# Experts with 64-column weight blocks as the stationary operand, and the ranking lists of units 20 to 23 in another buffer

## The chip, the cores and the metric

The kernel runs on one core of a Trainium2 chip. The metric is device time in microseconds (us): before the change the median of three runs is 560.91 us, from 559.71 to 563.14. Five engines work in parallel, each through its own queue of instructions in order: PE (matmuls; PEld is its load of the stationary operand), DVE, ACT and POOL (element work), and SP, which only starts transfers. Transfers run on 16 DMA engines. In a matmul a stationary operand (`lhsT`) of up to 128 columns is loaded into the array and a moving operand (`rhs`) streams past it, so that the output has as many partitions as the stationary operand has columns. All arrays here are float32.

## The reference, cut to what matters

```
for t in range(S):                       # attention, state of 40 x 40 for each batch and head
    y[t]  = r[t] @ state
    state = state * w[t] - (state @ a[t]) outer b[t] + v[t] outer k[t]
x = y as rows of 320, 3072 tokens
logits = x @ w_gate                      # 8 experts, top 1
probs  = softmax(logits); each token goes to its best expert with weight gate_w
for e in range(8):
    tok = tokens of expert e; if more than 80: the 80 with the greatest gate_w
    out[tok] = gate_w[tok] * (relu(x[tok] @ w1[e]) @ w2[e])     # w1: 320 x 1024, w2: 1024 x 320
all other rows of out are 0
```

## The kernel before, in words

**Attention.** The sequence is cut into 24 units (64 steps, two batches each). Each unit's work is recorded in a planner, `Plan`, which lists all instructions in an order by their estimated costs and due times; the list is then issued, so each engine's order is fixed. This stage fills the span up to about 425 us. Its matmuls are mostly blocks of 64 by 64 (`psv_go`, `u_go`, `score`): four of them, in the four quarters of the array, follow each other in the program. `gate` computes a unit group's expert weights, and `rows_go` (L817) writes the group's rows of x to DRAM.

**Ranking.** For each expert the 80 greatest gate weights are wanted. `extract` takes eight maxima at a time (L846, L848), `merge` joins sorted lists. `rank_late` treats units 20 and 21, `rank_last` units 22 and 23; each first turns the gate weights into a list of 256 columns, `pair_a` and `pair_b` (L824, L839), which before the change lie in the two buffers named `raww`. All buffers of attention and ranking belong to the pool `hold`; `tops`, `gates` and `ids` belong to `const`.

**Weights.** When `hold` has been given back, `wpool` takes its place, and SP starts the transfers of the eight experts one after the other (L978, L980, L981): `w1` (1024 KB), `w1r`, the last 64 of the 320 rows of w1, in two halves (2 x 128 KB), and `w2` (1280 KB). That is 20.97 MB for all; every expert has tiles of its own, so that no transfer waits for the experts' work.

**Choice of tokens.** L1010 to L1051 turn the lists into a threshold, and the threshold into each expert's 80 row numbers (`idx_g`, `idx_s`).

**Experts.** POOL gathers the rows of each expert (L1063). For each expert: `turn_x` transposes them (three PE transposes, L1074 and L1075, then a DVE copy to `xe`); `first_layer` has `xe` (80 columns) stationary and lets `w1` stream past in pieces of 512 columns, four matmuls over 128 rows (L1085) and two over 64 rows, in the upper and the lower half of the array (L1088), then ReLU on ACT; `turn_h` transposes h (80 x 1024) by eight PE transposes (L1100) and two DVE copies; `second_layer` has a piece of the turned h stationary and lets `w2` stream past, eight matmuls of 320 columns (L1108); DVE multiplies by the gate weight (L1110) and POOL scatters the rows to `out` (L1111). The tile framework decides the final order on each engine and puts in the waits.

Of the kernel before, what the change touches and what calls it, by code (L numbers as in the profile page):

```python
# [145 lines left out]
def kernel(  # L146
# [77 lines left out]
    with ExitStack() as p1:  # L224
# [599 lines left out]
        pair_a, pair_b = at("raww", NM), at("raww", NM + 1)  # L824
# [4 lines left out]
        def turn_gates(pieces, dst, key, z, bis):  # L829
            kc = ("gp", pieces[0][0])  # L830
            rows = pieces[0][1] * E

            def go():
                for j, (m0, nu) in enumerate(pieces):
                    nc.tensor.transpose(ps[0:rows, bank(kc), 128 * j : 128 * j + 128],
                                        gates[:, m0 : m0 + nu, :].rearrange("p m e -> p (m e)"), ident)
            addr("PE", 0.2 * len(pieces), 0.2, z, go, [("gates", b_) for b_ in bis], (), (kc, 1))
            addr("DVE", 0.25 + 0.001 * 128 * len(pieces), 0.1, z,
                lambda: nc.vector.tensor_copy(dst, ps[0:rows, bank(kc), 0 : 128 * len(pieces)]), [kc], [key])  # L839
# [55 lines left out]
        def rank_late():  # L895
            ranked.append(1)
            z = 22 * PER
            turn_gates([(20, 1), (21, 1)], pair_a[0:E, 0:256], ("raww", NM), z, [5])
            clear_tail(z)
            extract(la[0:E], pair_a[0:E, 0:256], z, ("raww", NM), LA)  # L900
            merge(8, tops[0], tops[0], z, A0, A0)

        def rank_last():
            ranked.append(1)
            z = 24 * PER
            turn_gates([(22, 1), (23, 1)], pair_b[0:E, 0:256], ("raww", NM + 1), z, [6])
            extract(tops[1], pair_b[0:E, 0:256], z, ("raww", NM + 1), ("tops", 1))
# [151 lines left out]
    rows, xes, hs, hts = {}, {}, {}, {}  # L1059
# [18 lines left out]

    def first_layer(e):
        w1, w1r, _ = weights[e]  # L1080
        xe = xes.pop(e)
        hp = [ps_h.tile([cap, FH], F32, name="hp", tag=f"h{j}") for j in range(2)]
        for i in range(2):
            for j in range(2):
                nc.tensor.matmul(hp[j], lhsT=xe[:, i, :], rhs=w1[:, i, FH * j : FH * j + FH], start=i == 0, stop=False)  # L1085
        for j in range(2):
            half = slice(64 * j, 64 * j + 64)
            nc.tensor.matmul(hp[j], lhsT=xe[half, 2, :], rhs=w1r[half, :], start=False, stop=True)  # L1088
        hs[e] = fs.tile([cap, F], F32, name="h", tag="h")
        for j in range(2):  # L1090
            nc.scalar.activation(hs[e][:, FH * j : FH * j + FH], hp[j], Act.Relu)  # L1091

    def turn_h(e):
        h = hs.pop(e)
        hts[e] = fs.tile([128, FK, cap], F32, name="hT", tag="hT")
        for j in range(2):
            tp = ps_t.tile([128, FK // 2, cap], F32, name="tp", tag=f"t{j}")
            for f in range(FK // 2):
                o = FH * j + 128 * f
                nc.tensor.transpose(tp[:, f, :], h[:, o : o + 128], ident[:cap, :cap])  # L1100
            nc.vector.tensor_copy(hts[e][:, FK // 2 * j : FK // 2 * (j + 1), :], tp)  # L1101

    def second_layer(e):
        w2 = weights[e][2]
        hT = hts.pop(e)
        yp = ps_y.tile([cap, DM], F32, name="yp", tag="y")
        for f in range(FK):
            nc.tensor.matmul(yp, lhsT=hT[:, f, :], rhs=w2[:, f, :], start=f == 0, stop=f == FK - 1)  # L1108
        y = fs.tile([cap, DM], F32, name="y", tag="y")
        nc.vector.tensor_scalar_mul(y, yp, rows[e][:, DM : DM + 1])  # L1110
# [7 lines left out]
    for e in range(E + 1):  # L1118
        if e < E:
            first_layer(e)  # L1120
        if e + 1 < E:
            turn_x(e + 1)
        if e > 0:
            second_layer(e - 1)
        if e < E:
            turn_h(e)
# [26 lines left out]
```

## Time and profile before

| | |
|---|---|
| median of three runs | 560.91 us |
| profiled execution: its own time | 561.64 us |
| its span, first to last instruction | 559.6 us |
| PE busy in the span | 425.6 us (76%) |
| mean granted TensorE clock | 0.891 |
| bytes moved in the span | 72.91 MB |

A row of a timeline begins with the start and the length in us; equal instructions that follow each other on an engine are put together with their count. One float32 matmul of the program stands in the trace as two matmul instructions, with a load each; a PE transpose stands as one. Matmuls overlap, and each has an own length of 0.2 us and more after its operand has begun to stream; so the pace of a stream is read from start to start, not from lengths. Numbers in square brackets in a row are idle time before it, and what ended that.

### The profile page before, as it was taken

How to read it: one execution, taken by the hardware profiler on the slowest of the kernel's cores; microseconds unless marked ns; L12 is line 12 of the kernel's file. 1: busy time of each engine (PE TensorE's matmuls, PEld its weight loads, DVE VectorE, ACT ScalarE, POOL GpSimd, SP SyncE). 2: the span in 40 equal slices, each digit the busy share in tenths (PEclk: the TensorE clock that was granted, in tenths of full speed). 3: DMA queues.
4: the chain of work that ended last, by engine and by line, in shares of the span. 5: the costliest groups of instructions: out<-in, count | busy, mean ns of one | idle time of the engine just before them, and what ended most of it. 6: DMA issues, size and time to landing. Idle time of an engine off the chain costs nothing. (4 is left out here: it accounts for less than half of the span.)

```text
span 559.6 us, 22079 instructions
## 1 busy us (share of the span) xinstructions
PE 425.6 (76%) x9617; PEld 331.6 (59%) x9617; DVE 312.5 (56%) x706; ACT 186.0 (33%) x361; POOL 224.1 (40%) x393
## 2 busy tenths in 40 slices
PE   2644089797928988889799998998895003999996
PEld 2543078686717877778687887887784002344443
DVE  4867977444703855684476644966678981121211
ACT  2432064353512453444443643445231000101010
POOL 7010011788388410898699516981000005010101
PEclk9978569798976999999899999999699555899999
DMA  8775367556593477676577374327200049999300
GB/s 133 113 116 112 64 154 133 99 94 133 96 243 81 99 174 134 149 132 117 133 143 172 100 132 116 75 44 161 71 16 27 23 143 342 326 332 344 104 15 16
DMA packets 241444, 72.91 MB, mean 130 GB/s; under 512 B 217908, under 2 KB 235716, under 8 KB 241348
## 3 DMA queue, kind: packets, MB, share of 16 engines
q1 hardware_dynamic: 211428, 65.50, 51.6%
q10 hardware_dynamic: 29152, 4.36, 4.9%
q0 software_dynamic: 768, 1.64, 1.0%
q8 instruction: 76, 1.25, 0.9%
q14 instruction: 20, 0.16, 0.1%
HBM read 53.26 MB, written 18.13 MB: 128 GB/s over the span
## 5 line engine op out<-in xcount | busy, mean ns | idle before, releaser
L498 POOL TENSOR_TENSOR tmp<-lt 128x30 f32<-128x30 f32 (+9 forms) x150 | 84.0, 560 | 61.0 <-DMA lt<-blocks 50.3
L500 POOL TENSOR_TENSOR lt<-lt,tmp 128x30 f32<-128x30 f32 (+9 forms) x150 | 88.8, 592 | 11.8
L707 DVE TENSOR_TENSOR UL<-ps,mask 128x832 f32<-128x832 f32 x24 | 24.5, 1022 | 54.0 <-PE ps L702 54.0
L758 PE MATMUL ps<-wsel,xT 128*128 128x192 f32 x192 | 40.7, 360 | 2.3 <-DVE xT L748 1.4
L1111 POOL DMA_INDIRECT out_dram<-y,idx_s x8 | 7.3, 917 | 74.6 <-DVE y L1110 74.6
L758 PEld LDWEIGHTS ps<-wsel,xT 128*128 128x128 f32 x192 | 34.2, 208 | 4.3 <-DVE xT L748 1.7
L369 DVE TENSOR_TENSOR_SCAN P<-dec,begins 128x520 f32<-128x520 f32 x24 | 31.4, 1313 | 9.4 <-ACT dec L365 9.3
L1108 PE MATMUL yp<-w,hT 128*80 128x320 f32 x128 | 35.9, 434 | 0.5 <-DVE hT L1101 0.5
L344 PE MATMUL ps<-ident,raww 128*128 128x128 f32 x88 | 16.6, 320 | 25.5 <-DMA raww<-in_w_dram 24.4
L344 PE MATMUL ps<-ident,kb 128*128 128x128 f32 x192 | 32.8, 297 | 3.6 <-DVE ends L373 1.8
L735 DVE TENSOR_TENSOR st<-ps,st 128x832 f32<-128x832 f32 (+1 forms) x24 | 23.8, 990 | 17.9 <-PE ps L724 17.9
L485 POOL MEMSET nt<- 32x1024 f32 x12 | 11.3, 945 | 54.6 <-ACT nt L417 54.2
L377 DVE TENSOR_TENSOR_SCAN iv<-dec,ends 128x520 f32<-128x520 f32 x24 | 30.2, 1259 | 4.0 <-ACT ivc L396 3.3
L1085 PE MATMUL hp<-w,xe 128*80 128x512 f32 x64 | 31.6, 641 | 0.5 <-DVE xe L1077 0.5
L452 DVE TENSOR_TENSOR psi<-ps,mask 128x512 f32<-128x512 f32 x24 | 16.4, 686 | 27.3 <-PE ps L437 23.0
L1091 ACT ACTIVATE h<-hp 80x512 f32<-80x512 f32 x16 | 8.6, 587 | 61.5 <-PE hp L1088 61.5
L611 ACT COPY rv<-ps 128x1024 f32<-128x1024 f32 x24 | 24.3, 1014 | 11.4 <-PE ps L344 6.5
L344 PEld LDWEIGHTS ps<-ident,raww 128*128 128x128 f32 x88 | 11.5, 162 | 27.4 <-DMA raww<-in_w_dram 15.1
L1108 PEld LDWEIGHTS yp<-w,hT 128*80 128x80 f32 x128 | 18.6, 150 | 14.7 <-issue 0.8
L344 PEld LDWEIGHTS ps<-ident,kb 128*128 128x128 f32 x192 | 22.8, 149 | 7.4 <-issue 3.7
L407 DVE TENSOR_TENSOR kb<-rawkb,ps 128x640 f32<-128x640 f32 x22 | 17.9, 813 | 15.5 <-PE ps L344 13.4
L1077 DVE COPY xe<-xp 128x240 f32<-128x240 f32 x8 | 3.3, 407 | 40.9 <-PE xp L1075 40.9
(171 smaller groups left out, 961.3 us busy)
## 6 DMA issues: line engine op xcount, KB each, us to landing
w<-in_moe_w_dram SPq DMA_DIRECT2D x8, 1280.0 KB
w<-in_moe_w_dram SPq DMA_DIRECT2D x8, 1024.0 KB, 16.4
VL<-in_v_dram SPq DMA_DIRECT2D x96, 40.0 KB, 2.3
out_dram<-zero SPq DMA_DIRECT2D x8, 480.0 KB, 4.2
raww<-in_w_dram SPq DMA_DIRECT2D x44, 80.0 KB, 2.8
rawkb<-in_k_dram SPq DMA_DIRECT2D x44, 80.0 KB, 3.6
rawkb<-in_b_dram SPq DMA_DIRECT2D x44, 80.0 KB, 3.2
rawr<-in_r_dram ACTq DMA_DIRECT2D x84, 40.0 KB, 2.9
```

The lines of the kernel that those rows point to most:

```text
L344: nc.tensor.matmul(o, lhsT=i, rhs=ident, start=True, stop=True, is_transpose=True, skip_group_check=True)
L369: nc.vector.tensor_tensor_scan(at("P", n), at("dec", n)[:, 0 : H * SEG], begins, 0.0, op0=Alu.mult, op1=Alu.add)
L377: nc.vector.tensor_tensor_scan(at("iv", n)[:, H * SEG : 0 : -1], at("dec", n)[:, H * SEG : 0 : -1], at("ends", n)[:, H * SEG : 0 : -1], 0. ...
L407: nc.vector.tensor_tensor(out=view(at("kb", n), 0, (HB * H, 2), (HB, H), (1, D)), in0=view(at("rawkb", n), 0, (DM, 2), (D, H), (1, D)), in ...
L498: e.tensor_tensor(out=tv, in0=t3[:, 0:s, s : s + 1].to_broadcast([128, s, n]), in1=t3[:, s : s + 1, s + 1 :].to_broadcast([128, s, n]), op ...
L500: e.tensor_tensor(out=t3[:, 0:s, s + 1 :], in0=t3[:, 0:s, s + 1 :], in1=tv, op=Alu.add)
L611: nc.scalar.copy(at("rv", n).rearrange("p (k c) -> p k c", k=2), ps[:, bank(kr) : bank(kr) + 2, :])
L707: nc.vector.tensor_tensor(out=view(at("UL", n), 0, (M4 * X, 2), (1, M4 * X)), in0=view(ps[:, bank(ku), :], 0, (512, 2), (1, M4 * X)), in1= ...
L735: nc.vector.tensor_tensor(out=view(st, o, (BS, M4), (step, 2), (1, n_)), in0=view(flat, 512 * bank(ky) + o, (4 * T, M4), (step, 2), (1, n_ ...
L758: nc.tensor.matmul(ps[:, b0, WS * m : WS * m + WX], lhsT=at("xT", n)[:, 2 * T * cof(m, 0) : 2 * T * cof(m, 0) + 2 * T], rhs=wsel_[:, WS * ...
L1085: nc.tensor.matmul(hp[j], lhsT=xe[:, i, :], rhs=w1[:, i, FH * j : FH * j + FH], start=i == 0, stop=False)
L1108: nc.tensor.matmul(yp, lhsT=hT[:, f, :], rhs=w2[:, f, :], start=f == 0, stop=f == FK - 1)
```

## The change

The two lists of units 20 to 23 now lie in `begins`, a constant of the attention stage that is no longer read by then; the copy into a list is recorded as a write of `begins`, too. In the experts the roles of the operands are exchanged: blocks of 64 columns of `w1`, `w1r` and `w2` are stationary, and `xe` (80 columns) or the turned h (80 columns) moves. Even blocks write partitions 0 to 63 of a PSUM tile, odd ones 64 to 127. The first layer then gives h already turned, so that `turn_h` goes; ReLU is now split between ACT (`hp[0]`) and DVE (`hp[1]`). The second layer gives y turned, and a new `turn_y` turns it back: a DVE copy to `yT`, two PE transposes, and one matmul with `pair`, two 64 x 64 identities above one another, which adds the two halves of y's last 64 columns (their even pieces are summed in one half, their odd ones in the other). `pair` is made by two POOL copies ahead of the gathers.

```diff
@@ -821,7 +821,7 @@
             add(*args, sooner=LISTS[len(ranked)], **kw)
 
         ranked = []
-        pair_a, pair_b = at("raww", NM), at("raww", NM + 1)
+        pair_a, pair_b = begins[:, 0:256], begins[:, 256:512]
 
         def clear_tail(z):
             addr("POOL", 0.4, 0.1, z, lambda: nc.gpsimd.memset(la[:, capr:], 0.0), (), [("la", 0)])
@@ -836,7 +836,8 @@
                                         gates[:, m0 : m0 + nu, :].rearrange("p m e -> p (m e)"), ident)
             addr("PE", 0.2 * len(pieces), 0.2, z, go, [("gates", b_) for b_ in bis], (), (kc, 1))
             addr("DVE", 0.25 + 0.001 * 128 * len(pieces), 0.1, z,
-                lambda: nc.vector.tensor_copy(dst, ps[0:rows, bank(kc), 0 : 128 * len(pieces)]), [kc], [key])
+                lambda: nc.vector.tensor_copy(dst, ps[0:rows, bank(kc), 0 : 128 * len(pieces)]), [kc],
+                 [key] + [("begins", 0)] * (key[0] == "pair"))
 
         def extract(dst, src, z, src_key, dst_key):
             cols = src.shape[-1]
...
@@ -895,16 +896,16 @@
         def rank_late():
             ranked.append(1)
             z = 22 * PER
-            turn_gates([(20, 1), (21, 1)], pair_a[0:E, 0:256], ("raww", NM), z, [5])
+            turn_gates([(20, 1), (21, 1)], pair_a[0:E, 0:256], ("pair", 0), z, [5])
             clear_tail(z)
-            extract(la[0:E], pair_a[0:E, 0:256], z, ("raww", NM), LA)
+            extract(la[0:E], pair_a[0:E, 0:256], z, ("pair", 0), LA)
             merge(8, tops[0], tops[0], z, A0, A0)
 
         def rank_last():
             ranked.append(1)
             z = 24 * PER
-            turn_gates([(22, 1), (23, 1)], pair_b[0:E, 0:256], ("raww", NM + 1), z, [6])
-            extract(tops[1], pair_b[0:E, 0:256], z, ("raww", NM + 1), ("tops", 1))
+            turn_gates([(22, 1), (23, 1)], pair_b[0:E, 0:256], ("pair", 1), z, [6])
+            extract(tops[1], pair_b[0:E, 0:256], z, ("pair", 1), ("tops", 1))
 
         def late_adds():
             def late_consts():
@@ -1056,7 +1057,10 @@
     ps_h = ctx.enter_context(tc.tile_pool(name="ps_h", bufs=2, space=PSUM))
     ps_t = ctx.enter_context(tc.tile_pool(name="ps_t", bufs=1, space=PSUM))
     ps_y = ctx.enter_context(tc.tile_pool(name="ps_y", bufs=1, space=PSUM))
-    rows, xes, hs, hts = {}, {}, {}, {}
+    rows, xes, hts, yts = {}, {}, {}, {}
+    pair = fs.tile([128, HB], F32, name="pair", tag="pair", bufs=1)
+    nc.gpsimd.tensor_copy(pair[0:HB], ident[0:HB, 0:HB])
+    nc.gpsimd.tensor_copy(pair[HB:], ident[HB:, HB:])
 
     def gather(e):
         rows[e] = fs.tile([cap, XW], F32, name="rows", tag="rows", bufs=8)
@@ -1076,38 +1080,48 @@
         xes[e] = fs.tile([128, 3, cap], F32, name="xe", tag="xe")
         nc.vector.tensor_copy(xes[e], xp)
 
+    QF, NB = FK // 2, FH // 64
+
     def first_layer(e):
         w1, w1r, _ = weights[e]
         xe = xes.pop(e)
-        hp = [ps_h.tile([cap, FH], F32, name="hp", tag=f"h{j}") for j in range(2)]
+        hp = [ps_h.tile([128, QF, cap], F32, name="hp", tag=f"h{j}") for j in range(2)]
         for i in range(2):
             for j in range(2):
-                nc.tensor.matmul(hp[j], lhsT=xe[:, i, :], rhs=w1[:, i, FH * j : FH * j + FH], start=i == 0, stop=False)
-        for j in range(2):
-            half = slice(64 * j, 64 * j + 64)
-            nc.tensor.matmul(hp[j], lhsT=xe[half, 2, :], rhs=w1r[half, :], start=False, stop=True)
-        hs[e] = fs.tile([cap, F], F32, name="h", tag="h")
-        for j in range(2):
-            nc.scalar.activation(hs[e][:, FH * j : FH * j + FH], hp[j], Act.Relu)
-
-    def turn_h(e):
-        h = hs.pop(e)
+                for b in range(NB):
+                    c = 64 * (b % 2)
+                    nc.tensor.matmul(hp[j][c : c + 64, b // 2, :], lhsT=w1[:, i, FH * j + 64 * b : FH * j + 64 * b + 64],
+                                     rhs=xe[:, i, :], start=i == 0 and b < 2, stop=False, skip_group_check=True)
+        for b in range(NB):
+            c = 64 * (b % 2)
+            for j in range(2):
+                half = slice(64 * j, 64 * j + 64)
+                nc.tensor.matmul(hp[j][c : c + 64, b // 2, :], lhsT=w1r[half, 64 * b : 64 * b + 64],
+                                 rhs=xe[half, 2, :], start=False, stop=True, skip_group_check=True)
         hts[e] = fs.tile([128, FK, cap], F32, name="hT", tag="hT")
-        for j in range(2):
-            tp = ps_t.tile([128, FK // 2, cap], F32, name="tp", tag=f"t{j}")
-            for f in range(FK // 2):
-                o = FH * j + 128 * f
-                nc.tensor.transpose(tp[:, f, :], h[:, o : o + 128], ident[:cap, :cap])
-            nc.vector.tensor_copy(hts[e][:, FK // 2 * j : FK // 2 * (j + 1), :], tp)
+        nc.scalar.activation(hts[e][:, 0:QF, :], hp[0], Act.Relu)
+        nc.vector.tensor_scalar_max(hts[e][:, QF:, :], hp[1], 0.0)
 
     def second_layer(e):
         w2 = weights[e][2]
         hT = hts.pop(e)
-        yp = ps_y.tile([cap, DM], F32, name="yp", tag="y")
+        yp = ps_y.tile([128, 3, cap], F32, name="yp", tag="y", bufs=2)
         for f in range(FK):
-            nc.tensor.matmul(yp, lhsT=hT[:, f, :], rhs=w2[:, f, :], start=f == 0, stop=f == FK - 1)
+            for b in (0, 1, 2, 3, 4) if f % 2 == 0 else (1, 0, 3, 2, 4):
+                c = 64 * ((b + f) % 2) if b == 4 else 64 * (b % 2)
+                nc.tensor.matmul(yp[c : c + 64, b // 2, :], lhsT=w2[:, f, 64 * b : 64 * b + 64], rhs=hT[:, f, :],
+                                 start=f == 0 and b < 2, stop=f >= (FK - 2 if b == 4 else FK - 1), skip_group_check=True)
+        yts[e] = fs.tile([128, 3, cap], F32, name="yT", tag="yT")
+        nc.vector.tensor_copy(yts[e], yp)
+
+    def turn_y(e):
+        yT = yts.pop(e)
+        yq = ps_t.tile([cap, DM], F32, name="yq", tag="yq")
+        for i in range(2):
+            nc.tensor.transpose(yq[:, 128 * i : 128 * i + 128], yT[:, i, :], ident)
+        nc.tensor.matmul(yq[:, KW:], lhsT=yT[:, 2, :], rhs=pair, start=True, stop=True, skip_group_check=True)
         y = fs.tile([cap, DM], F32, name="y", tag="y")
-        nc.vector.tensor_scalar_mul(y, yp, rows[e][:, DM : DM + 1])
+        nc.vector.tensor_scalar_mul(y, yq, rows[e][:, DM : DM + 1])
         nc.gpsimd.indirect_dma_start(
             out=out[:, :], out_offset=bass.IndirectOffsetOnAxis(ap=idx_s[:, e : e + 1], axis=0),
             in_=y[:, :], element_offset=0, bounds_check=N - 1, oob_is_err=False, in_offset=None)
@@ -1120,10 +1134,11 @@
             first_layer(e)
         if e + 1 < E:
             turn_x(e + 1)
+        if e > 1:
+            turn_y(e - 2)
         if e > 0:
             second_layer(e - 1)
-        if e < E:
-            turn_h(e)
+    turn_y(E - 1)
 
 
 # ---- launch: one core; inputs and outputs as the reference has them ----
```

The scheduler's order on PE (before, around the second expert): the operands' names stand after the operation, `w_1` is w1 of expert 1, `x4` a count of matmuls, and "waits" names the semaphores of the engines or transfers that are waited for.

```order
L1085 MATMUL hp<-w_1_7002,xe 80x512 [waits DMAHW5_49,DVE_49]
L1085 MATMUL hp<-w_1_7002,xe 80x512 x3
L1088 MATMUL hp<-w1r_7003,xe 80x512 [waits DMAHW6_49]
L1088 MATMUL hp<-w1r_7003,xe 80x512 [waits DMAHW7_49]
L1074 MATMUL xp<-ident,rows 128x80 [waits DMASW2_49,PE_49]
L1074 MATMUL xp<-ident,rows 128x80
L1075 MATMUL xp<-ident,twice 128x80
L1108 MATMUL yp<-w_0_6997,hT 80x320 [waits DMAHW4_49,DVE_49]
```

And in the changed kernel, for the fourth and fifth expert:

```order
L1093 MATMUL hp<-xe,w_3_7016 64x80 x31
L1099 MATMUL hp<-xe,w1r_7017 64x80 [waits DMAHW6_49]
L1099 MATMUL hp<-xe,w1r_7017 64x80 [waits DMAHW7_49]
L1099 MATMUL hp<-xe,w1r_7017 64x80 x14
L1078 MATMUL xp<-ident,rows 128x80 [waits DMASW4_49,PE_49]
L1078 MATMUL xp<-ident,rows 128x80
L1079 MATMUL xp<-ident,twice 128x80 [waits Activation_49]
L1121 MATMUL yq<-ident,yT 80x128 [waits DVE_49]
L1121 MATMUL yq<-ident,yT 80x128
L1122 MATMUL yq<-pair,yT 80x64
L1112 MATMUL yp<-hT,w_2_7011 64x80 [waits DMAHW4_49,Activation_49]
L1112 MATMUL yp<-hT,w_2_7011 64x80 x39
```

A first layer is now 32 + 16 matmuls of 64 x 80 and a second layer 40, with the turns of the next x and an earlier y between them. For the later experts the scheduler lays a first layer in the midst of an earlier second layer; all matmuls are there once.

On SP, where the first transfer of weights is released (rows with - are of the kernel before, rows with + of the change; `w_0` in L978 is w1 of expert 0):

```order
 L817 DMA x_rows<-xg_139 128x2x321 [waits DMAHW0_49,Activation_49,Pool_49]
-L978 DMA w_0_6995<-in_moe_w_dram 128x2x1024 [waits DMAHW2_49,DMAHW1_49,DMAHW3_49,DMAHW0_49,DMAHW4_49,DVE_49,DMAHW6_49,PE_49,DMAHW7_49,Activation_49,Pool_49]
-L980 DMA w1r_6996<-in_moe_w_dram 64x512 x2
-L981 DMA w_0_6997<-in_moe_w_dram 128x8x320
+L979 DMA w_0_6995<-in_moe_w_dram 128x2x1024 [waits DMAHW2_49,DMAHW1_49,DMAHW3_49,DMAHW0_49,DMAHW4_49,DVE_49,DMAHW6_49,PE_49,DMAHW7_49,Activation_49,Pool_49]
+L981 DMA w1r_6996<-in_moe_w_dram 64x512 x2
+L982 DMA w_0_6997<-in_moe_w_dram 128x8x320
```

Nothing moved here but line numbers. In both programs the count of DVE that is waited for is 621, that of the last maximum written to the list of units 22 and 23 (L846 before, L847 in the change).

On POOL, ahead of the gathers:

```order
+L1001 MEMSET seg 128x8 [waits Pool_49]
+L1062 COPY pair<-ident 64x64 [waits PE_49,DVE_49,Activation_49,Pool_49]
+L1063 COPY pair<-ident 64x64
+L1067 DMA rows<-x_rows,idx_g 80x321 [waits Pool_49]
+L1067 DMA rows<-x_rows,idx_g 80x321 x7
```

The copies of `pair` now carry the wait for DVE that the first gather had, and the gathers stand behind them.

## Rows read from the trace of the kernel before

**Rows 1.** The page's slices: the span in 40 equal parts, tenths of full.
```profile
PEclk9978569798976999999899999999699555899999
DMA  8775367556593477676577374327200049999300
```

**Rows 2.** Stretches: length, busy us of each engine (instructions), granted clock, DMA share, GB/s.
```profile
440.00:450.00 10.00, 0.59 (x2) 0.09 (x2) 9.59 (x44) 0.00 (x0) 0.42 (x2) 0.50 0.09 33
460.00:470.00 10.00, 2.13 (x24) 1.83 (x24) 3.29 (x9) 0.00 (x0) 3.85 (x4) 0.50 1.07 342
470.00:480.00 10.00, 7.56 (x13) 2.58 (x15) 0.41 (x1) 1.17 (x6) 3.62 (x4) 0.56 1.06 311
490.00:500.00 10.00, 10.00 (x42) 4.70 (x41) 1.75 (x4) 1.35 (x4) 0.95 (x1) 1.00 1.06 351
530.00:540.00 10.00, 10.00 (x45) 4.80 (x44) 1.85 (x5) 1.07 (x2) 0.91 (x1) 1.00 0.03 10
```

**Rows 3.** Timeline from the last maximum to the first expert: start, length, instruction.
```profile
453.46 0.42 DVE L846 MAX8 tops<-raww 8x8 f32<-8x256 f32 x1
...
454.08 0.37 SPq L978 DMA_DIRECT2D w<-in_moe_w_dram  x1
...
465.16 1.13 POOL L1063 DMA_INDIRECT rows<-x_rows,idx_g  x1 [10.09 <-DVE idx_s L1051]
...
471.94 0.50 PE L1074 MATMUL xp<-ident,rows 80*128 80x80 f32 x2 [8.40 <-DMA rows<-x_rows,idx_g]
...
473.24 6.43 PE L1085 MATMUL hp<-w,xe 128*80 128x512 f32 x8 [0.50 <-DVE xe L1077]
```

**Rows 4.** Timeline of PE over one expert of the steady stretch.
```profile
491.87 3.60 PE L1085 MATMUL hp<-w,xe 128*80 128x512 f32 x8
495.40 1.09 PE L1088 MATMUL hp<-w1r,xe 64*80 64x512 f32 x4
496.42 0.36 PE L1074 MATMUL xp<-ident,rows 80*128 80x80 f32 x2
...
496.68 4.47 PE L1108 MATMUL yp<-w,hT 128*80 128x320 f32 x16
500.99 0.72 PE L1100 MATMUL tp<-ident,h 80*128 80x80 f32 x8
501.55 1.02 PE L1085 MATMUL hp<-w,xe 128*80 128x512 f32 x2
```

**Rows 5.** Timeline of the end.
```profile
550.37 4.54 PE L1108 MATMUL yp<-w,hT 128*80 128x320 f32 x16 [0.48 <-DVE hT L1101]
...
554.95 0.55 DVE L1110 TENSOR_SCALAR y<-yp,rows 80x320 f32<-80x320 f32 x1 [4.23 <-PE yp L1108]
...
555.77 0.91 POOL L1111 DMA_INDIRECT out_dram<-y,idx_s  x1 [4.67 <-DVE y L1110]
```

**Rows 6.** Stretches of 1 us where the weights' transfers end, columns as in Rows 2.
```profile
522.00:523.00 1.00, 1.00 (x3) 0.30 (x2) 0.00 (x0) 0.00 (x0) 0.28 (x1) 1.00 0.41 129
523.00:524.00 1.00, 1.00 (x4) 0.30 (x2) 0.00 (x0) 0.00 (x0) 0.00 (x0) 1.00 0.19 53
524.00:525.00 1.00, 1.00 (x6) 0.22 (x4) 0.00 (x0) 0.00 (x0) 0.00 (x0) 1.00 0.00 0
```

**Rows 7.** Timeline of PE in the dense attention stage, 64 x 64 blocks.
```profile
258.06 0.89 PE L702 MATMUL ps<-W,nt 64*64 64x104 f32 x32
258.77 0.64 PE L437 MATMUL ps<-ah,kT 64*64 64x64 f32 x32
```

**Rows 8.** Groups by line and shape: count, busy us, mean ns, idle time before.
```profile
L306 POOL COPY gt<-ident 32x256 f32<-32x256 f32 x2 | 0.8, 392 | 0.1
...
L809 POOL COPY xg<-gsm 128x2 f32<-128x2 f32 x2 | 0.4, 192 | 34.6 <-issue 23.4 <-DVE gsm L806 11.3
...
L1077 DVE COPY xe<-xp 128x240 f32<-128x240 f32 x8 | 3.3, 407 | 40.9 <-PE xp L1075 40.9
L1091 ACT ACTIVATE h<-hp 80x512 f32<-80x512 f32 x16 | 8.6, 587 | 61.5 <-PE hp L1088 61.5
```

## The prediction

> **What bounds the kernel now.** I read the slices of the page first, then stretches of ten microseconds, then the timeline. The slices [rows 1] show TensorE's clock dropping at about three quarters of the span and returning, and the transfers idle just before they rise to full load: one phase ends there and another begins. The stretches [rows 2] say what each is bound by. From 440 to 450 DVE is busy 9.59 of 10 us: the ranking. [...] From 490 PE is busy 10.00 of 10 us at the full clock, and from 530 to 540 still, when the transfers have ended (10 GB/s). So the last 85 us are: choice of tokens, a gather, and then PE alone. The timeline [rows 3] gives the way in: last maximum 453.46 to 453.88, first weight transfer 454.08, first gather issued 465.16, its rows on PE at 471.94, first layer from 473.24. One expert in the steady stretch [rows 4] is 9.68 us (491.87 to 501.55) with no gap: first layer 3.53, its 64-row part 1.02, turn of x 0.26, second layer 4.31, turn of h 0.56. The end [rows 5]: the last matmul ends at 554.91 and the span at 559.6, 4.69 us for the multiplication, the scatter's issue and its landing. The weights land by 523.3 or so (129, 53 and 0 GB/s in three successive microseconds [rows 6]), over 30 us before PE is done, so they do not bound the end.
>
> **The ranking's lists.** I cost the move at nothing, and as a gain at nothing either. The copies and maxima are the same in number, shape and order, only their buffer differs. By the order on SP the first weight transfer waits for the same thing before and after: DVE's count 621, the last maximum of the last list. It is released when the whole pool is done with, not when the two buffers are. Transfers therefore begin at 454.1 again [rows 3].
>
> **Making `pair`.** Two POOL copies of 64 x 64 now stand between DVE's last row number and the first gather, on the path to the first expert. This trace has POOL copies of 0.19 (2 columns) and 0.39 us (256 columns, 32 partitions) [rows 8]; I take 0.45 us for both (0.4 to 0.8). First matmul of the experts: 473.24 + 0.45 = 473.7.
>
> **One expert on PE.** The unit is one matmul instruction with 80 moving columns. Eight turns of h of exactly that width take 0.56 us from start to start, 70 ns each [rows 4]; the second layer's instructions of 320 columns take 4.31 / 16 = 269 ns, 67 ns for each 80 columns, so the pace follows the columns that stream and the loads lie beside it. I take 70.
>
> The new blocks are 128 rows by 64 columns, so a matmul alone would use half of the array. The question on which all hangs is whether even and odd blocks run side by side. The trace has no 128 x 64 blocks. The nearest are the attention's 64 x 64 blocks, in all four quarters: 32 instructions of 104 columns start within 0.71 us (258.06 to 258.77 [rows 7]), 22 ns each, where 104 columns at the pace above are 91 ns. Four at a time would be 23 ns: quarters overlap fully, two of them over the same rows, and their loads of 64 columns are hidden. The other end is no overlap: 70 ns each. I take pairs, 35 ns, since in the program odd and even blocks alternate throughout, and since the nearest row shows full overlap.
>
> - first layer, main part: 32 matmuls, 64 instructions, 32 pairs x 70 ns = 2.24 us
> - 64-row part: 16 matmuls, 32 instructions in fours, 8 x 70 ns = 0.56
> - second layer: 40 matmuls, 80 instructions, 40 pairs x 70 ns = 2.80
> - turn of x as before: 0.26
> - turn of y: two turns of 128 columns (112 ns each) and one matmul of 64 columns (2 x 56 ns) = 0.34; the turn of h (0.56) is gone
> - change of block shape: 3.53 us for eight instructions of 512 columns (8 x 431 ns = 3.45) and 1.02 for two pairs of such (0.86) leave 0.08 on entering and 0.16 on leaving the 64-row blocks [rows 4]. The new order changes shape about four times per expert: 0.45 (0.24 to 0.8).
>
> The sum is 6.65 us against 9.68. DVE and ACT stay covered: per expert DVE has the copy of xe (0.41 [rows 8]), a ReLU, a copy of y turned, each about as wide, and the multiplication (0.55 [rows 5]), 1.8 us; ACT's ReLU shrinks from two of 0.59 [rows 8] to one.
>
> [...] First the row: in the second layer loads of 80 columns over all 128 rows take no time beyond the stream (269 ns for 320 columns) [rows 4]. [...]
>
> **The sum.** 473.7 + 8 x 6.65 less one turn of x that lies ahead = 526.6. The clock: it is at its lower level when the experts begin and rises amid the first layer (mean 0.56 from 470 to 480 [rows 2]); that layer's main part took 6.43 us there [rows 3] against 3.60 later [rows 4], and I take the same loss, 2.8 us. Waits that nothing covers: the first second layer waits for ReLU (0.4), and the last two turns of y each wait for the copy to `yT` (0.4 of copy and a start, 0.5 each): 1.4. Last matmul at 530.8, plus 4.69: span 535.5. The same reckoning for the kernel before (473.24 + 8 x 9.68 - 0.26 + 2.8 + its last wait of 0.48 [rows 5]) gives 553.7 against 554.9 in the trace. The profiled execution has 561.64 us for a span of 559.6, so 2.04 around it: 537.5. It lies 0.73 above the median, so on the median's scale 536.8. I forecast **537 us**, 24 less (4.3%).
>
> What is late next: the weights. At 20.97 MB over 455 to 523.3 the last `w2` (a sixteenth of all) lands about 523.3, and my sum starts the last second layer at 527.1. Were PE faster than I think, the end could not come before 523.3 + 2.8 + 0.9 (copy and turn) + 4.69 = 531.7 of span, 533 on the median's scale.
>
> **Rivals.**
> 1. *Overlap is partial.* If the 0.16 us behind the 64-row part is no change of shape but what two tiles lose (0.86 of 1.02 is 0.84), pairs cost 70 / 0.84 = 83 ns, 41 each: 144 instructions x 8 experts x 6.5 ns = 7.5 us more, **544**. For it: no two blocks over all rows have been seen together. Against: full overlap of quarters [rows 7]. Chance 0.18. [...]
> 2. *Slower: 64-column blocks over 128 rows don't overlap, or their loads are exposed.* Then the 144 instructions per expert of both layers' main parts (1152 in all) follow each other in one line, at 70 ns instead of 35: 40 us more, **577**. A load's price is unknown, between 0 and 70 ns (turns of h load 128 columns within a 70 ns step [rows 4]); at 35 ns in each half-array a pair takes 105 ns, 53 each, and the time is 557. It decides from 56 ns per instruction upward: there the 24 us are eaten. For it: operands of 80 columns leave little to hide a load behind, where 320 and 512 did. Against: hidden loads at 104 columns [rows 7]. Chance 0.11 for slower, 0.06 for the middle.
> 3. *Weights bind* (PE at 6 us per expert): 533. This lies within the forecast's own range.
> 4. *The lists do what the title says* and transfers begin at the last x, about 11 us earlier, between 440 and 450. The order on SP speaks against it. It would be worth 1 us at most, since in my sum PE hardly waits for weights: 536. Chance 0.05, inside the forecast.
>
> **Numbers.** Forecast with its bounds (533 to 541: pair copies, shape changes, waits) 0.65; rival 1 (541 to 550) 0.18; near today's time 0.06; slower 0.11. The range that leaves out two in ten reaches from 532 to 550. A measurement of this kernel can tell about 1% from no change. Faster by over 1%: 0.83; within: 0.06; slower: 0.11.
>
> **What would show it.** Starts of L1093 and L1112 35 ns apart on average in the steady stretch, two by two; 6.65 us per expert; the first transfer of weights within 1 us of 454; the first layer near 473.7; the clock at its full level before the first expert's layer ends; PE with no idle time longer than 0.6 us after that. Wrong are: steps of 60 ns or more in L1112 (rival 2), idle time of PE ended by transfers of w (rival 3), a clock that falls back amid the experts.

## The result

The changed kernel takes 553.03 us (median of four runs, 551.70 to 559.79) against 561.52 for the kernel before beside it (four runs, 559.71 to 563.14): ratio 0.989, interval 0.9845 to 0.9942. The medians lie 8.5 us apart, where 24 us were forecast, the ratio says 0.6 to 1.6%, and the time lies above the forecast's range (532 to 550). The profiled execution has 551.7 us, for a span of 549.9.

The slices of the page after (PEclk and DMA as in [rows 1]) show a clock that never settles while the transfers run:

```profile
PEclk9978569898976998999899998999699755788898
DMA  8676367577693587676676485315410009999900
```

The stretches of ten microseconds (columns as in [rows 2]):

```profile
480.00:490.00 10.00, 7.03 (x173) 6.43 (x177) 1.21 (x3) 0.78 (x3) 0.00 (x0) 0.93 1.06 355
490.00:500.00 10.00, 8.46 (x212) 7.79 (x213) 1.84 (x4) 0.83 (x3) 0.95 (x1) 0.90 1.06 330
500.00:510.00 10.00, 9.25 (x176) 8.60 (x179) 2.02 (x5) 1.21 (x5) 0.94 (x1) 0.83 1.07 312
510.00:520.00 10.00, 7.48 (x148) 6.51 (x145) 2.31 (x5) 0.44 (x1) 0.98 (x2) 0.83 1.07 325
530.00:540.00 10.00, 9.49 (x262) 8.77 (x257) 2.32 (x5) 0.88 (x2) 0.91 (x1) 1.00 0.05 14
```

Before, PE was busy 10.00 of 10 us from 490 at the full clock [rows 2]. Now it is busy 7 to 9 us, and at a clock of 0.83 to 0.93, as long as the DMA share is above 1; with the transfers over (530 to 540) the clock is full. The timeline of PE says what the gaps are (number in brackets: idle time before the row, and what ended it):

```profile
484.28 0.92 PE L1093 MATMUL hp<-xe,w 128*64 128x80 f32 x21
487.59 2.33 PE L1093 MATMUL hp<-xe,w 128*64 128x80 f32 x42 [2.39 <-issue]
489.85 1.35 PE L1099 MATMUL hp<-xe,w1r 64*64 64x80 f32 x32
...
500.75 0.35 PE L1099 MATMUL hp<-xe,w1r 64*64 64x80 f32 x3 [2.04 <-issue]
...
515.43 1.23 PE L1112 MATMUL yp<-hT,w 128*64 128x80 f32 x19 [2.52 <-issue]
...
527.93 2.44 PE L1093 MATMUL hp<-xe,w 128*64 128x80 f32 x63
530.30 0.78 PE L1099 MATMUL hp<-xe,w1r 64*64 64x80 f32 x32
531.01 2.01 PE L1112 MATMUL yp<-hT,w 128*64 128x80 f32 x50
```

The gaps lie inside loops (a first layer stops after 21 of its instructions, 484.28, and goes on 2.39 us later), and no data are waited for: "issue" means that the profile shows nothing that the engine waited for. Behind the long ones PE runs at half clock: 32 instructions of the 64-row part take 1.28 us at 489.85 (to 491.13, clock 0.50), but 0.71 at 530.30 (to 531.01, clock 1.00). After 522 there is no such gap.

In front of the experts little moved (rows picked out of a timeline, as [rows 3]):

```profile
452.04 0.42 DVE L847 MAX8 tops<-begins 8x8 f32<-8x256 f32 x1
452.66 0.37 SPq L979 DMA_DIRECT2D w<-in_moe_w_dram  x1
462.97 0.23 POOL L1062 COPY pair<-ident 64x64 f32<-64x64 f32 x1 [9.32 <-DVE idx_s L1052]
463.83 1.13 POOL L1067 DMA_INDIRECT rows<-x_rows,idx_g  x1 [0.36 <-POOL pair L1063]
470.36 0.50 PE L1078 MATMUL xp<-ident,rows 80*128 80x80 f32 x2 [8.24 <-DMA rows<-x_rows,idx_g]
```

The first weights start 0.62 us after the start of the last maximum, as before (454.08 - 453.46), and the first gather 11.79 us after it (11.70 before). They end where the forecast had them, if one counts from the last maximum (columns as in [rows 6]):

```profile
521.00:522.00 1.00, 1.00 (x30) 0.93 (x26) 0.00 (x0) 0.00 (x0) 0.00 (x0) 1.00 0.73 233
522.00:523.00 1.00, 0.86 (x34) 0.68 (x32) 0.00 (x0) 0.00 (x0) 0.00 (x0) 1.00 0.10 36
```

**How the kernels are compared below.** The time ahead of the last maximum differs between profiled executions, from 452.0 to 463.4 us, although the attention's instructions are the same (the four kernels with early transfers, e6, e7, e8 and e11, have 459.1 to 463.4, the ten others 452.0 to 457.9). So beside the median I read two pieces of each profile: from the last maximum to the first turn of x (choice of tokens, gather), and from there to the end of the span (the experts). These two pieces come from one profiled execution each. All in us; n is the number of runs. The ratios and their intervals leave out the runs that fell into a slower state of the chip, the medians do not.

| kernel | median (n) | ratio to before, same chip | last maximum to first x | first x to end |
|---|---|---|---|---|
| before | 561.52 (4) | | 18.48 | 87.7 |
| changed | 553.03 (4) | 0.989 [0.9845, 0.9942] | 18.32 | 79.5 |
| e1 lists only | 564.91 (10) | 1.003 [0.9982, 1.0078] | 18.31 | 87.6 |
| e2 one expert's weights | 536.68 (4) | 0.954 [0.9457, 0.9618] | 14.78 | 63.5 |
| e3 its weights, all transfers | 556.76 (10) | 0.989 [0.9843, 0.993] | 18.91 | 79.1 |
| e4 128-column blocks | 630.24 (4) | 1.119 [1.111, 1.1274] | 18.50 | 154.1 |
| e5 first layer only | 549.05 (4) | 0.978 [0.9682, 0.9878] | 18.33 | 71.9 |
| e6 changed, early transfers | 555.83 (4) | 0.989 [0.9772, 1.0012] | 18.40 | 75.5 |
| e7 first layer only, early | 553.58 (10) | 0.986 [0.981, 0.9902] | 18.20 | 71.6 |
| e8 mix of 5 and 3, early | 548.06 (4) | 0.980 [0.9678, 0.993] | 18.24 | 68.7 |
| e9 two wide first layers | 551.95 (1) | | 18.29 | 74.3 |
| e10 mix of 6 and 2 | 546.36 (4) | 0.973 [0.9642, 0.981] | 18.46 | 69.7 |
| e11 e8 again | 550.74 (4) | 0.980 [0.9714, 0.9891] | 18.37 | 68.9 |
| e12 changed again | 557.14 (10) | 0.991 [0.9863, 0.996] | 18.33 | 80.9 |

By this measure the change gave 8.2 us in the experts (87.7 to 79.5), and the forecast for that piece was 63.1 (535.5 less 472.4).

### The profile page after: what moved, and what is told of

Read it like the earlier page. It is cut to its first block, busy times and chain, and to the rows that moved or that the text cites. A ratio compares the mean times of both kernels' runs of the same rounds, so it can differ in the third digit from the quotient of the medians.

```text
span 549.9 us, 24379 instructions
## 1 busy us (share of the span) xinstructions
PE 408.9 (74%) x10769; PEld 354.5 (64%) x10769; DVE 313.4 (57%) x706; ACT 181.1 (33%) x353; POOL 225.1 (41%) x395
## 5 line engine op out<-in xcount | busy, mean ns | idle before, releaser
L498 POOL TENSOR_TENSOR tmp<-lt 128x30 f32<-128x30 f32 (+9 forms) x150 | 81.2, 541 | 64.6 <-DMA lt<-blocks 53.9
L500 POOL TENSOR_TENSOR lt<-lt,tmp 128x30 f32<-128x30 f32 (+9 forms) x150 | 91.4, 609 | 11.8
L1112 PE MATMUL yp<-hT,w 128*64 128x80 f32 x640 | 29.2, 247 | 3.0 <-issue 2.8
L452 DVE TENSOR_TENSOR psi<-ps,mask 128x512 f32<-128x512 f32 x24 | 16.4, 688 | 25.6 <-PE ps L437 22.1
L1112 PEld LDWEIGHTS yp<-hT,w 128*64 128x64 f32 x640 | 26.3, 147 | 4.7 <-issue 3.3
L689 ACT COPY W<-ps 128x832 f32<-128x832 f32 x24 | 20.5, 854 | 15.8 <-PE ps L684 8.1
L655 PE MATMUL ps<-VL,psi 64*64 64x104 f32 x768 | 24.9, 270 | 0.6 <-DVE VL L628 0.3
L1093 PE MATMUL hp<-xe,w 128*64 128x80 f32 x512 | 22.5, 247 | 3.7 <-issue 3.2
```

Source lines behind the costliest of these rows:

```text
L498: e.tensor_tensor(out=tv, in0=t3[:, 0:s, s : s + 1].to_broadcast([128, s, n]), in1=t3[:, s : s + 1, s + 1 :].to_broadcast([128, s, n]), op ...
L500: e.tensor_tensor(out=t3[:, 0:s, s + 1 :], in0=t3[:, 0:s, s + 1 :], in1=tv, op=Alu.add)
L655: nc.tensor.matmul(ps[T * x : T * x + T, b0 + q, X * i : X * i + X], lhsT=psi[rows, q, i, :], rhs=at("VL", n)[rows, vo : vo + X], start=i ...
L1093: nc.tensor.matmul(hp[j][c : c + 64, b // 2, :], lhsT=w1[:, i, FH * j + 64 * b : FH * j + 64 * b + 64], rhs=xe[:, i, :], start=i == 0 and ...
L1112: nc.tensor.matmul(yp[c : c + 64, b // 2, :], lhsT=w2[:, f, 64 * b : 64 * b + 64], rhs=hT[:, f, :], start=f == 0 and b < 2, stop=f >= (FK ...
```

## The experiments

My theory (**supply**): PE's instructions do not arrive fast enough while the weights fill the DMA engines. The list of queues of the changed kernel, in the stretch of the gap at 484.9 to 487.6, has one transfer of instructions among 707 packets of weights (queue, kind: packets, MB, share of the 16 engines):

```profile
q1 hardware_dynamic: 707, 0.91, 104.6%
q8 instruction: 1, 0.02, 2.7%
```

Transfers of this kind (16384 bytes each) start at 478.02, 484.99, 491.68, 498.31, 505.21, 512.83 and 520.16, and after the weights at 523.71, 528.18, 532.21, 537.25 and 542.76. The five gaps up to 520 that are longer than 0.2 us end (at 480.58, 487.59, 494.34, 500.75 and 515.43) 2.56, 2.60, 2.66, 2.44 and 2.60 us after the start of such a transfer. An expert now has 183 matmul instructions with a load each, 366, where it had 39 and 39. Up to 520 one transfer comes in 7.0 us (42.14 / 6). At 256 instructions a transfer an expert is then supplied in 366 / 256 x 7.0 = 10.0 us: the old pace (9.68), whatever the blocks do. The 256 is worked out from the traces (PE has 21732 records in the whole trace of the changed kernel for 85 such transfers, 255.7 each, and 19432 for 76 before, 255.7 too). Beside full DMA engines the trace has 8.0 us of idle time ended by issue, without the traffic none (e2, below).

The rivals: PE waits for weights, though the profile does not say so (e2 against e3); the paired blocks themselves suffer from the transfers (e5); the loads of 64 columns are to blame, and fewer, wider blocks would do (e4).

**e1.** The kernel before with the lists moved, experts unchanged.

```diff
-pair_a, pair_b = at("raww", NM), at("raww", NM + 1)
+pair_a, pair_b = begins[:, 0:256], begins[:, 256:512]
...
```

> The kernel before with the first half of the change alone: lists of units 20 to 23 in `begins`, experts as before. My reading of the order says that the first transfer of weights still waits for the last maximum: transfers begin within 1 us of its end, as before, and the time is that of the kernel before within 0.5% (558 to 564 us). If the lists' place mattered, transfers would begin about 11 us earlier, right after the last write of x rows; the time would still be the same, since PE and not the transfers bounds the old experts.

Measured: no difference (564.91 us, 0.9 above the range that I gave, where the kernel before beside it has 562.64; ratio 1.003), and the first transfer still follows the last maximum (456.99 after 456.38). The lists' part of the change does nothing.

**e2 and e3.** All experts use expert 0's weights. e2 (shown) transfers only these; e3 keeps the two lines that load all eight, 21 MB, and adds the last two.

```diff
-    for e in range(E):
-        load_expert(e)
+    load_expert(0)
+    for e in range(1, E):
+        weights[e] = weights[0]
```

> The changed kernel, but all experts use expert 0's weights and only these (2.6 of 21 MB) are transferred, so the output is another. Supply theory (PE runs out of instructions, since their transfers of 16 KB, 256 instructions, come only every 6.9 us while weights fill the DMA engines, and PE uses 256 in some 4.7 us): no idle time of PE over 0.3 us ended by issue after the first expert, full clock throughout, 534 to 540 us. Rival W (PE waits for weights that have not landed): the same, 534 to 540. Rival P (the stalls come from the order of PE's own work, the change of block shapes or the clock): stalls stay, about 550.

> As the one before (all experts use expert 0's weights, the output is another), but all 21 MB are transferred as in the changed kernel; seven eighths are never read. Supply theory: the traffic is what hurts, so PE stalls as in the changed kernel, 8 us in all before the transfers end, and the time is 549 to 556. Rival W: no wait for weights is left, 534 to 540. Rival P: about 550.

A stretch of e2, columns as above, and rows picked out of one of its experts:

```profile
510.00:520.00 10.00, 10.00 (x289) 9.75 (x285) 2.10 (x6) 0.44 (x1) 1.82 (x2) 1.00 0.09 24
```

```profile
489.60 2.99 PE L1113 MATMUL yp<-hT,w 128*64 128x80 f32 x80
492.42 2.38 PE L1094 MATMUL hp<-xe,w 128*64 128x80 f32 x64
494.73 0.78 PE L1100 MATMUL hp<-xe,w1r 64*64 64x80 f32 x32
495.44 0.36 PE L1079 MATMUL xp<-ident,rows 80*128 80x80 f32 x2
496.15 2.99 PE L1113 MATMUL yp<-hT,w 128*64 128x80 f32 x80
```

Three of the gaps of e3's timeline (rows picked out):

```profile
489.95 3.06 PE L1095 MATMUL hp<-xe,w 128*64 128x80 f32 x41 [2.55 <-issue]
503.16 0.23 PE L1101 MATMUL hp<-xe,w1r 64*64 64x80 f32 x1 [2.23 <-issue]
517.79 0.78 PE L1114 MATMUL yp<-hT,w 128*64 128x80 f32 x16 [2.67 <-issue]
```

The same instructions run without a gap at the full clock when nothing is transferred, and stop again when the transfers run beside them, though seven eighths of what is transferred is never read. So it is the transfers, not the weights' arrival. (e3's median, 556.76 us, lies 0.8 above the range that I gave.) In e2 the experts take 63.5 us, and the forecast's own sum was 63.1. The changed kernel's 16.1 us more are idle time of PE (9.9 us from the first turn of x to the last matmul, 1.2 in e2: 8.7 more) and a longer busy time (7.4 more), which the sums over these stretches show, the changed kernel first:

```profile
470.36:545.00 74.64, 63.88 (x1464) 58.36 (x1464) 14.19 (x32) 6.44 (x24) 8.92 (x10) 0.90 0.75 229
472.03:531.00 58.97, 56.48 (x1464) 53.43 (x1464) 13.62 (x32) 6.08 (x24) 11.55 (x13) 0.94 0.11 28
```

Where the gaps stand says more than when they end. Counted in matmuls and loads in the trace, the gaps of the changed kernel stand 254 instructions apart (once 508: there PE had run at half clock from 502.2 to 505.6 and came to the block's end later), those of e3 254 to 256 and those of e12, below, 252 to 256, in whichever loop PE is. No loop of the program has this length; a block of instructions has it (255.7 on average, as counted above). And after each of the five gaps the next such transfer starts only 4.0 to 4.7 us after PE has gone on, while in e2 it starts within 0.6 us of PE's passing the same counts. With the 2.4 to 2.7 us from that start to PE's going on, a block takes about 7 us to come, and PE is through with one in 4.6 us (254 at the 366 in 6.55 us of e2). What is left is 2.4 us, the length of the long gaps.

**e4.** Blocks of 128 columns in place of pairs of 64, half the instructions, in both layers (the main part of the first is shown).

```diff
-for b in range(NB):
-    c = 64 * (b % 2)
-    nc.tensor.matmul(hp[j][c : c + 64, b // 2, :], lhsT=w1[:, i, FH * j + 64 * b : FH * j + 64 * b + 64],
+for b in range(QF):
+    nc.tensor.matmul(hp[j][:, b, :], lhsT=w1[:, i, FH * j + 128 * b : FH * j + 128 * b + 128],
...
```

> The changed kernel with stationary blocks of 128 columns in place of pairs of 64 (last 64 columns of the second layer still in 64-column blocks): the same result, the same streamed columns on PE (a 128-column block of 70 ns in place of two 64-column blocks side by side), but 103 in place of 183 matmul instructions, and as many loads, per expert. Supply theory: 206 instructions per expert need 5.6 us at 256 per 6.9 us, less than PE's 6.65, so stalls all but vanish: 534 to 541. Rival W: weights are as late as before, stalls stay, about 550. Rival P: unclear for shapes, but the scheduler's interleaving stays: about 550; if loads of 128 columns don't hide behind 80 moving ones, slower than the changed kernel, 560 and more.

I had this far wrong: 630 us. There is no gap ended by issue, as the supply theory has it (a transfer of instructions comes only every 19 to 26 us here), but the time says nothing about the theory: PE is busy 10.00 of 10 us at half clock from its first expert to the end:

```profile
489.03 7.03 PE L1092 MATMUL hp<-xe,w 128*128 128x80 f32 x32
496.00 2.00 PE L1097 MATMUL hp<-xe,w1r 64*128 64x80 f32 x16
```

6.97 us for 32 steps are 218 ns each (213 from start to start within the row), for 80 columns that take 70 ns at the full clock.

**e9**, run later, takes this apart: the kernel of e5 (next), with such blocks only in the main part of the first layers of experts 6 and 7.

> The kernel with the first layer alone turned round, and the main part of the first layer of experts 6 and 7 in blocks of 128 columns instead of pairs of 64 (32 instructions in the place of 64). The all-128 kernel had steps of 213 ns at the clock's lower level from its first expert to the end. If the step is the load of 128 columns that 80 moving columns do not cover, it is half of that here, 107 ns at the full clock, and the main part takes 32 x 0.107 = 3.4 us instead of 2.4. If the step is what 80 columns take (70 ns), 2.2 us, and the 213 ns had another cause. What the clock does in that stretch (begun at full) shows whether such blocks hold it or lower it; the layers behind show whether it stays.

```profile
514.43 2.44 PE L1099 MATMUL hp<-xe,w 128*64 128x80 f32 x64
516.79 0.78 PE L1105 MATMUL hp<-xe,w1r 64*64 64x80 f32 x32
...
522.08 3.69 PE L1094 MATMUL hp<-xe,w 128*128 128x80 f32 x32
525.71 0.78 PE L1105 MATMUL hp<-xe,w1r 64*64 64x80 f32 x32
```

At the full clock a 128-column step takes 112 ns (from start to start; 3.63 us for 32), a pair of 64-column blocks, the same work, 74 (2.36 us for 32 pairs). The experts of e9 (one run) take 2.4 us more than those of e5 (74.3, 71.9), and 2 x (3.63 - 2.36) is 2.5. What makes the difference is not shown. I took it for the load of 128 columns, not covered by 80 moving ones, but no run varies the moving columns against the load, and the turns of h before, with a load of 128 columns (over 80 rows) and 80 moving ones, have steps of 70 ns [rows 4]. The 213 ns at half clock (e4) are 1.9 times the 112. Why the clock stays low through all of e4 is not settled: in e9 it held 1.00 through both stretches of 3.6 us.

**e5.** Only the first layer with weights stationary; the second layer is the old one, 16 instructions of 320 columns, and h needs no turn. `second_old` is the second layer of the kernel before, without its copies of h.

```diff
+    OLD = E - 0
...
-            second_layer(e - 1)
+            (second_old if e <= OLD else second_layer)(e - 1)
```

> The changed kernel, but only the first layer has its weights stationary; the second layer is that of the kernel before (16 instructions of 320 columns, no turn of y). Theory S (PE's instructions arrive too slowly while the weights' transfers run, about 256 matmuls and loads per 6.9 us): an expert has 115 matmuls and 115 loads, 230 instead of 366, so 6.2 us of supply against some 8.0 us of work (first layer 2.37, its 64-row part 0.71, turn of x 0.26, second layer 4.31, changes of shape 0.4). So no idle time of PE ended by issue longer than 1 us, clock at full from the second expert on, and 473.2 + 8 x 8.0 + 2.8 - 0.3 + 0.4 + 4.7 + 2 = 547 (544 to 550): faster than the changed kernel's 553 though each expert is slower on paper. Rival R (paired blocks themselves suffer from the transfers, in their loads or their operands): the first layers, half of the paired instructions, still stall, half of the changed kernel's loss: 552 to 556, with stalls inside L1093.

Its timeline, one expert in the midst of the transfers (DMA share 1.07):

```profile
491.49 2.43 PE L1093 MATMUL hp<-xe,w 128*64 128x80 f32 x64
493.86 0.79 PE L1099 MATMUL hp<-xe,w1r 64*64 64x80 f32 x32
494.57 0.36 PE L1078 MATMUL xp<-ident,rows 80*128 80x80 f32 x2
494.77 0.23 PE L1079 MATMUL xp<-ident,twice 80*128 80x80 f32 x1
494.83 4.47 PE L1134 MATMUL yp<-w,hT 128*80 128x320 f32 x16
499.24 2.43 PE L1093 MATMUL hp<-xe,w 128*64 128x80 f32 x64
```

No gap ended by issue here, 2.37 us for the first layer's main part (2.31 in e2, without transfers), 7.75 us per expert, so that 256 instructions last 8.6 us, longer than a block takes to come. On paper an expert here is 1.2 us slower than the changed one (6.55 in e2); in fact the experts take 71.9 us instead of 79.5. So pairs do not suffer from the transfers, the number of instructions does. The rival falls.

**e6 and e7.** Transfers from the last x, with the changed experts and with those of e5: the buffers that the ranking still uses are moved from the pool `hold` to `const`, so that `hold` can be given back earlier.

```diff
-        begins = hold.tile([128, H * SEG], F32, name="begins")
...
-        cd, la, lb, lc = (hold.tile([128, 128], F32, name=name) for name in ("cd", "la", "lb", "lc"))
+        cd = hold.tile([128, 128], F32, name="cd")
...
+    la, lb, lc = (const.tile([128, 128], F32, name=name) for name in ("la", "lb", "lc"))
+    begins = const.tile([128, H * SEG], F32, name="begins")
```

> The changed kernel, with the ranking's buffers (la, lb, lc, begins) moved to the pool that lives to the end, so that the attention pool is given back at the last x and the first weights' transfer starts near 443.7 instead of 453. Theory S: the transfers end near 513 instead of 522, the stalls end with them; of the 16 us that the changed kernel loses to the one without traffic (553 against 537) over 49 us of overlap, 9 us less overlap gives back about 3: 549 to 551. If the stalls had another cause than the transfers, 553 as before. If the transfers slow the choice of tokens (its instructions and the gathers), it loses 1 to 3 us before 472 and ends at 551 to 554.

> Both: transfers from the last x, and only the first layer with stationary weights. Theory S: where nothing stalls, the earlier transfers give nothing: the time of the kernel with the first layer alone, within 2 us (545 to 549). If that kernel has stalls left, or a wait for weights, it gains up to 4 us.

Here transfers do begin ahead of the last maximum, by 7.7 us (451.47 and 459.17 in e6). The experts of e6 gain 4.0 us (79.5 to 75.5; 3 were expected), and the gaps end with the transfers, the last at 522.45, the transfers between 521 and 522. The experts of e7, which had no gaps, gain nothing (71.6 against 71.9). In size this is what the supply theory has. But the gain of e6 lies in PE's busy time (60.4 us for 63.9) and not in its idle time (9.5 for 9.9); against the second profile of the changed kernel (e12) it is 5.4 us, 3.2 of them idle time. So e6 alone doesn't show the mechanism. The medians I missed, by nearly 5 us each: the attention ended later in these profiles (last maximum at 459.2 and 463.4). All four kernels with the moved buffers have it late, later than any of the ten others, and e7's median lies 4.5 us above that of e5, on the same chip. So the move itself probably costs some 5 us ahead of the experts; how, no run shows.

**e8, e10 and e11: few instructions while transfers run, many afterwards.** The second layer is the old one for experts 0 to 4 (e8, e11, with early transfers) or 0 to 5 (e10, without, OLD = E - 2), the new one for the others.

```diff
-    OLD = E - 0
+    OLD = E - 3
```

> Transfers from the last x; experts 0 to 4 with the first layer alone turned round, experts 5 to 7 with both layers. Theory S: the transfers end near 513, while the fifth expert is worked on, so the last three experts run at their full pace of 7.5 instead of 8.0 to 8.2 us and their instructions are not late: 1.5 to 2 us below the kernel with the first layer alone, less the turn of y at the end (0.9): 544 to 547. If it is not faster than that kernel, instructions of the last three are late too or the end's turn costs what they gain.

> The first layer turned round for all experts, the second layer turned round for the last two experts only; weights as in the changed kernel. Theory S: the transfers are over, or nearly, when the last two second layers run, so that they take 3.0 + 0.5 instead of 4.3 us each, and the turn of y at the end costs 0.9: from the last maximum to the end 90.2 - 1.6 + 0.9 = 89.5, within 1 us of the kernel with the first layer alone; 0.972 to 0.982 of before.

> The kernel with transfers from the last x and both layers turned round in the last three experts, again, to be compared with the two others on one chip: 0.974 to 0.984 of before, 87 us from the last maximum to the end, and faster than the changed kernel by 5 to 8 us.

> The changed kernel itself, beside the two candidates: 0.985 to 0.994 of before; each stall of PE ended by issue ends 2.4 to 2.7 us after the start of a transfer of instructions, as in its first profile.

Both mixes are faster than either kernel (e8 took 548.06 us, 1 above the range that I gave). e10 is the fastest: 546.36 us, ratio 0.973, where the changed kernel beside it on the same chip (e12) has 557.14 and 0.991. Their runs don't touch: 545.14 to 547.47 and 554.57 to 563.33. That e10 is faster than e5, too, is less sure: its experts take 2.2 us less (69.7, 71.9) in one profile of each, and the intervals of the two ratios overlap. PE in e10, stretches as above:

```profile
490.00:500.00 10.00, 10.00 (x190) 7.49 (x187) 1.37 (x4) 0.78 (x4) 1.76 (x2) 1.00 1.07 347
510.00:520.00 10.00, 10.00 (x126) 6.47 (x126) 1.35 (x3) 0.44 (x1) 0.91 (x1) 1.00 1.06 326
520.00:530.00 10.00, 10.00 (x179) 7.60 (x179) 1.90 (x4) 0.44 (x1) 1.82 (x2) 1.00 0.55 158
```

In e12 seven gaps ended by issue lie between 480 and 526, and each ends 2.42 to 2.72 us after the start of a transfer of instructions. Its PE is idle for 12.7 us, and the clock fell behind one of the gaps alone (0.50 from 519.6 to 523.0).

## Why the prediction was wrong

- **Lists: right.** Nothing gained, nothing lost (e1).
- **Copies of `pair`: 0.45 forecast, 0.1 measured** (11.79 against 11.70 us from the start of the last maximum to the first gather).
- **Pairs: right.** Steps of 37 ns on average in L1093 (2.37 us for 64 in e5; 2.31 and 36 in e2) and 35 in the second layer (2.82 for 80, 489.60 to 492.42 in e2, where the line is L1113), two by two: starts of L1093 in the changed kernel at 528.615, 528.621, 528.684, 528.690. The loads over all 128 rows, whose records last 137 ns each on average (L1093 and L1112 of the changed kernel, 527 to 541), lie beside the matmuls at these steps, and rivals 1 and 2 fall.
- **An expert: 6.65 forecast, 6.55 in e2** (489.60 to 496.15). The terms were small (2.24, 0.56, 2.80, 0.34 against 2.31, 0.71, 2.82, 0.44), since part of what I had put under changes of shape (0.45) lies in them.
- **Start, weights' end, DVE and ACT: right**, within a microsecond each, counted from the last maximum (to the first layer 19.6 us, forecast 20.2).
- **The tail: too small by 1.1.** From the last matmul to the end the changed kernel takes 5.8 us (544.13 to 549.92) and e2 as much, where 4.69 were forecast. In the changed kernel the last scatter is issued 1.04 us after the multiplication has ended, before the change 0.27; why is not shown. So it is in part luck that e2's 63.5 us come so near to the forecast's 63.1: its tail is 1.1 longer, its eight experts are 0.8 shorter.
- **The step that failed** stands under "The sum", in "Waits that nothing covers: ... 1.4": waits were counted for data only, and "I take the same loss, 2.8 us" let the clock be low once. Missing is a term for instructions. By the sum PE would start 366 of them in 6.65 us; they came, while the transfers ran, at 256 in 7.0 us. That made 8.0 of the 8.7 us of idle time, by groups of instructions over the experts (idle time last, and how much of it ended by issue):

```profile
L1112 PE MATMUL yp<-hT,w 128*64 128x80 f32 x640 | 29.2, 247 | 3.0 <-issue 2.8 <-ACT hT L1102 0.2
L1093 PE MATMUL hp<-xe,w 128*64 128x80 f32 x512 | 22.5, 247 | 3.7 <-issue 3.2 <-DVE xe L1081 0.5
L1099 PE MATMUL hp<-xe,w1r 64*64 64x80 f32 x256 | 7.5, 250 | 2.2 <-issue 2.0
```

The clock then fell behind the gaps of 2.39, 2.04 and 2.52 us (0.61 of full from 487.6 to 492, 0.67 from 500.8 to 506, 0.74 from 515.5 to 522). From the first turn of x on, PE was at 0.50 for 14.8 us, in e2 for 6.6; that is 4.1 of the 7.4 us of longer busy time. Another 1.2 or so lie at the six gaps (0.2 us each, as e3 against e2 has it): the last matmul ahead of a gap counts as busy up to its modelled end. Some 2 us are not accounted for; the scheduler's order on PE differs a little from e2's. So 8.7 us of idle time and 7.4 of busy time make up 16.1 of the 16.4 us by which the forecast for the experts was off (63.1 for 79.5). I had written "a clock that falls back amid the experts" down as a sign of error, but had no mechanism for it, and none of my four rivals was about instructions.
- What could have been read: the queues of the trace before have two transfers of instructions from 476 to 522, the changed kernel seven, and in the same stretch q1 fills the engines:

```profile
q1 hardware_dynamic: 8459, 14.54, 101.4%
q8 instruction: 2, 0.03, 0.3%
```

Nothing there shows that seven would be too many; but a count that grows 4.7 times on the engine that sets the end, on a resource at 101%, deserved a rival.

## What to carry to other kernels

Here cutting matmuls into more and smaller instructions (366 an expert for 78) cost supply, 8.0 us of idle time beside full DMA engines: count instructions per microsecond, and in such a stretch hold them below what the trace shows to arrive (here 256 in 7.0 us). Put the form with few instructions beside the transfers and the form with many behind them (e10). Compare stages, not totals, when an earlier stage varies by more than the effect.

## What was unexpected of the hardware

- With the DMA engines full, transfers of instructions came every 6.6 to 7.6 us; without (e2) every 4.0 to 5.1 us from 482.6 on, and PE had no gap. Each transfer itself lasts 1.07 to 1.25 us in the one case and 0.93 to 1.41 in the other, so its own length is not the difference. The start is late (4.0 to 4.7 us after PE has gone on, within 0.6 in e2); what delays it is not shown.
- The gather, too, pays for the transfers: 18.3 us from the last maximum to the first x, 14.8 in e2, 18.9 in e3.
- Two 64-column blocks side by side beat one of 128 columns (74 against 112 ns at the full clock in e9); why is not shown.
- PE, busy without a gap, stayed at the lower clock in e4 (0.50 in every stretch of ten that I read, from 480 to 610).
